# First gate weights of the second token half: raw and combined, into strided free rows of arena H instead of W

## The chip, the cores and the metric

One core of one Trainium2 chip. The metric is the device time of a run in microseconds (us). A time is quoted as the median of several runs, and a profile is one execution out of them.

## The reference, cut to what matters

```
xn = layernorm(A_x)                            # 2048 tokens x 1024
s  = linear_attention(xn, wqkv) @ wo           # 32 heads
g  = silu((silu(xn @ w_gate) * (xn @ w_up)) @ w_down)     # 1024 -> 3584 -> 1024
return A_x + s * g
```

The kernel does all large products with a Strassen-like scheme of seven multiplications, which needs sums and differences of weight blocks. VectorE makes these while TensorE multiplies. The tokens are worked in two halves of 1024.

## The kernel before

Each weight panel is loaded by `wload`: a raw panel of 8 KB per partition, four large sums of it ("combined"), and eight small sums for the inner level of the scheme.

```python
def wload(src, joint, dt=BF16, rd=()):
    s = raw_ring.take()
    dma(list(rd), [s.r], s.ap(dt).rearrange("p (kt n) -> p kt n", n=512), src, dsem("wr%d" % s.k), 1024 * KB)
    v = s.ap(dt).rearrange("p (kt w n) -> p w kt n", w=2, n=256)
    c = cmb_ring.take()
    ...
    sums({...}, [cv[:, q] for q in range(4)], [s.r], cr)        # four large sums
    ...
    for m in joint:                                              # m = 1, 5
        t = in_ring.take()
        ...
        sums(A, [tv[:, q] for q in range(4)], [r], tr)           # four small sums each
```

The buffers lie in arenas: W (52 KB), H (84 KB, the hidden activations), X, P, TM. At the turn from the first token half to the second, the last part of the first half's down projection ("d1") still reads its weights from W, while the first q panel ("q0"), gate panel ("g0") and up panel of the second half must come in:

```python
WD_AT = (((W, 0), (W, 35 * KB), (W, 7 * KB), None), ((W, 14 * KB), (W, 21 * KB), (W, 0), (W, 35 * KB)))
...
raw_ring.__init__([(X, 0), (W, 16 * KB), (W, 0), (X, 0), ...], 8 * KB)        # q0, g0, u0, ...
cmb_ring.__init__([(X, 8 * KB), (W, 28 * KB), (X, 8 * KB)] + ..., 8 * KB)
```

So g0's raw place, W 16 to 24 KB, is taken by d1's weights at 14 and 21 KB until d1's seventh multiplication. The order of instructions on every engine is fixed when the program is built: a planner schedules all operations with modelled durations, and each engine then runs its list in order.

Of the kernel before, what the change touches and what calls it, by code (L numbers as in the profile page):

```python
# [12 lines left out]
BF16 = mybir.dt.bfloat16  # L13
FP16 = mybir.dt.float16
KB = 1024
# [304 lines left out]
def build_kernel(nc, A_x, A_wqkv, A_wo, B_w_gate, B_w_up, B_w_down, out, WINDOW=6, NWARM=15, NPE=2, LEAD=12.0):  # L320
    S, D, FF = 2048, 1024, 3584
    NT, KT, NG, NPAIR = 16, 8, 8, 14
# [5 lines left out]
    wg_v = B_w_gate.rearrange("(kt p) f -> p kt f", p=128)  # L328
    wu_v = B_w_up.rearrange("(kt p) f -> p kt f", p=128)
# [3 lines left out]
    with ExitStack() as es:  # L333
# [20 lines left out]
        def named(*key):  # L354
            return Region([key])

        H = Arena("H", 84 * KB)
        X = Arena("X", 28 * KB)
        P = Arena("P", 16 * KB)
        W = Arena("W", 52 * KB)  # L360
# [50 lines left out]
        def sem(name):  # L411
            return es.enter_context(nc.semaphore(name))
# [4 lines left out]
        def dsem(name):  # L417
            if name not in semn:
                semn[name] = sem("d_" + name)
            return semn[name]  # L420
# [8 lines left out]
        def pe_mm(reads, writes, mms):  # L429
            return PL.op("pe", reads, writes, partial(_mm_group, mms), mm_cost(mms))  # L430
# [21 lines left out]
        def tt(reads, writes, o, a, b, op, fast=False):  # L452
            return dve(reads, writes, lambda h: h.tensor_tensor(o, a, b, op), nel(o), 1.92 if fast else 0.96)  # L453

        def dma(reads, writes, o, i, s, nbytes, cow=None, after=None):
            return PL.op("sp", reads, writes, lambda h: h.dma_start(o, i), 0.47, sem=s,  # L456
                         nbytes=nbytes * (1.45 if nbytes in (128 * KB, 896 * KB) else 1.0), cow=cow,
                         after=after)
# [97 lines left out]
        def combos(v, after=None):  # L556
            for o, a, b in (("T3", "R11", "R01"), ("T1", "R01", "R00"), ("T2", "R11", "T1"), ("T4", "R10", "T2")):
                for h in range(2):
                    w = {}
                    for nm in (o, a, b):  # L560
                        ap, r = v[nm]
                        n = len(r.keys) // 2
                        w[nm] = ap[:, 2 * h:2 * h + 2, :], Region(r.keys[n * h:n * h + n])
                    q = tt([w[a][1], w[b][1]], [w[o][1]], w[o][0], w[a][0], w[b][0], ALU.subtract, True)
                    if after is not None:
                        q.preds.add(after)
                        after.succs.append(q)
# [8 lines left out]
        for n in range(NWARM):  # L576
            b = n % 8
            m = 512 if n > 3 else 128
# [379 lines left out]
        for n, (fn, args) in enumerate(((x_load, (0,)), (x_load, (1,)), (wkv_load, (0, 1, 0)), (wkv_load, (0, 1, 1)),  # L958
# [3 lines left out]
            k = len(PL.ops)  # L962
# [6 lines left out]
        for n in range(6):  # L969
            o = pe_mm(wz_r[:1], [bank_r[kvb[2]]], [(ps[kvb[2]][:, 0:128], wz[:, 0:128], wz[:, 0:128], True, True)])  # L970
# [74 lines left out]
        for q, kb in enumerate(kvb):  # L1045
            n = 3 if q < 2 else 2
            src = ps[kb][:, 0:129 * n].rearrange("p (g n) -> p g n", n=129)[:, :, 128:129]
# [3 lines left out]
        for g in range(NG):  # L1051
            kvp = kv_ap(g)
            dve([bank_r[kvb[g // 3]], zi_r, mask_r], [H.reg(32 * KB + g * 256, 256)],
                lambda h, g=g, kvp=kvp: h.scalar_tensor_tensor(
                    KVZ[:, g, :], kvp[:, 0:128], zinv[:, g:g + 1], maskbd[:, :], ALU.mult, ALU.mult), 128)
# [35 lines left out]
        raw_ring = Places([(W, o * KB) for o in (0, 8, 16)], 8 * KB)  # L1091
        cmb_ring = Places([(W, 24 * KB), (W, 32 * KB)] * 2 + [(W, 24 * KB), (P, 0)] + [(W, 32 * KB), (W, 24 * KB)] * 6, 8 * KB)
        in_ring = Places([(W, 40 * KB), (W, 42 * KB), (W, 44 * KB), (TM, 8 * KB)], 2 * KB)

        def sums(A, o, rd, wr):

            tt(rd, [wr[0]], o[0], A[0, 1], A[1, 1], ALU.add, True)
            tt(rd + [wr[0]], [wr[1]], o[1], o[0], A[0, 0], ALU.subtract, True)
            tt(rd, [wr[2]], o[2], A[0, 0], A[0, 1], ALU.subtract, True)
            tt(rd + [wr[1]], [wr[3]], o[3], A[1, 0], o[1], ALU.subtract, True)  # L1100
# [1 line left out]
        RAW_OF = {1: (0, 0), 2: (1, 0), 4: (1, 1)}  # L1102
        SUM_OF = {5: 0, 6: 1, 7: 2, 3: 3}

        def wload(src, joint, dt=BF16, rd=()):


            s = raw_ring.take()
            dma(list(rd), [s.r], s.ap(dt).rearrange("p (kt n) -> p kt n", n=512), src, dsem("wr%d" % s.k), 1024 * KB)
            v = s.ap(dt).rearrange("p (kt w n) -> p w kt n", w=2, n=256)  # L1110
            c = cmb_ring.take()
            cv = c.ap(FP16).rearrange("p (m w kt n) -> p m w kt n", m=4, w=2, n=128)
            cr = [c.sub(q * 2 * KB, 2 * KB).r for q in range(4)]
            sums({(k, i): v[:, :, 4 * k:4 * k + 4, i * 128:i * 128 + 128] for k in range(2) for i in range(2)},
                 [cv[:, q] for q in range(4)], [s.r], cr)

            def block(m):
                if m in RAW_OF:
                    k, i = RAW_OF[m]
                    return v[:, :, 4 * k:4 * k + 4, i * 128:i * 128 + 128], s.r  # L1120
                return cv[:, SUM_OF[m]], cr[SUM_OF[m]]

            def stat(w, m):
                bl, r = block(m)
                return [bl[:, w, q, :] for q in range(4)], r
            inner = {}
            for m in joint:
                bl, r = block(m)
                t = in_ring.take()
                tv = t.ap(FP16).rearrange("p (m kt n) -> p m kt n", m=4, n=128)  # L1130
                tr = [t.sub(q * KB // 2, KB // 2).r for q in range(4)]
                A = {(k, i): bl[:, i, 2 * k:2 * k + 2, :] for k in range(2) for i in range(2)}
                sums(A, [tv[:, q] for q in range(4)], [r], tr)
                inner[m] = (A, r, tv, tr)

            def jstat(m, k):
                A, r, tv, tr = inner[m]
                if k in RAW_OF:
                    return [A[RAW_OF[k]][:, q, :] for q in range(2)], r
                return [tv[:, SUM_OF[k], q, :] for q in range(2)], tr[SUM_OF[k]]  # L1140
            return stat, jstat
# [116 lines left out]
                tt([sr, zrr], [sr], dst, src, zr, ALU.mult, True)  # L1258


        HB = 6 * KB
        HOF = {"R00": 0, "R10": 1, "R01": 2, "T1": 2, "R11": 3, "T2": 4, "T3": 5}

        def hb(n, nm):
            o = n * HB + HOF[nm] * KB
            return H.at(o, KB, FP16), H.reg(o, KB)

        def hb2(n, nm):

            v = H.at(n * HB, 2 * HB, FP16).rearrange("p (n b t) -> p n b t", n=2, t=512)[:, :, HOF[nm], :]  # L1270
            return v, Region(hb(n, nm)[1].keys + hb(n + 1, nm)[1].keys)

        def gu_load(k, n):
            return wload((wg_v if k == "g" else wu_v)[:, :, n * 512:(n + 1) * 512], (1, 5))

        sgs = {}

# [34 lines left out]
        def h_sums(n):  # L1312
            v = {nm: hb2(n, nm) for nm in HOF}
            tt([v["R11"][1], v["R01"][1]], [v["T3"][1]], v["T3"][0], v["R11"][0], v["R01"][0], ALU.subtract, True)
            tt([v["R01"][1], v["R00"][1]], [v["T1"][1]], v["T1"][0], v["R01"][0], v["R00"][0], ALU.subtract, True)
            tt([v["R11"][1], v["T1"][1]], [v["T2"][1]], v["T2"][0], v["R11"][0], v["T1"][0], ALU.subtract, True)
# [24 lines left out]
        def hq(nm, k, j, u0, u1):  # L1341

            v = H.at(0, NPAIR * HB, FP16).rearrange("p (u k b t) -> p u k b t", k=2, b=6, t=512)
            keys = []
            for u in range(u0, u1):
                keys += H.reg((2 * u + k) * HB + HOF[nm] * KB + j * 512, 512).keys
            return v[:, u0:u1, k, HOF[nm], j * 256:j * 256 + 256], Region(keys)

# [336 lines left out]
        gate = [0]  # L1685
# [16 lines left out]
        def turn_pass():  # L1702

            for q in range(4):
                dma([named("xscr", q)], [P.reg(q * 4 * KB, 4 * KB)], P.at(q * 4 * KB, 4 * KB, FP16), x_scr[q],
                    dsem("xl%d" % q), 512 * KB)
            k = len(PL.ops)
            combos(XV[1])
            x_inner(XV[1])
            for o in PL.ops[k:]:  # L1710
                o.urgent = 6.0
            gate[0] = 1
            raw_ring.__init__([(X, 0), (W, 16 * KB), (W, 0), (X, 0), (W, 8 * KB), (W, 16 * KB)] + [(W, 0), (W, 8 * KB), (W, 16 * KB)] * 5, 8 * KB)
            cmb_ring.__init__([(X, 8 * KB), (W, 28 * KB), (X, 8 * KB)] + [(W, 24 * KB), (W, 32 * KB)] * 8, 8 * KB)
            in_ring.__init__([(W, 14 * KB), (TM, 8 * KB), (W, 24 * KB), (W, 26 * KB), (W, 42 * KB), (W, 44 * KB)]
                             + [(W, 40 * KB), (TM, 8 * KB), (W, 42 * KB), (W, 44 * KB)] * 8, 2 * KB)
            pump(1)
            last_pair[0] = q_pair(1, 0, got["q", 1, 0], {}, False)
            return last_pair[0]
# [104 lines left out]
```

## Time and profile before

| | before |
|---|---|
| median of 3 runs | 712.3 us (711.97 to 712.69) |
| the profiled run | 713.57 us, span 711.8 us |
| TensorE busy | 705.0 us, 99% |
| VectorE busy | 630.9 us, 89% |

In the lines of a profile, PE is TensorE, DVE is VectorE, SPq is the queue that issues transfers, and "ps" is a PSUM buffer, into which TensorE's products go. The chain of that profile, in order of time (start, length, what), has its last two long TensorE pieces here:

```profile
349.45 29.75 PE ps L309 x175
...
416.46 228.48 PE ps L309 x1370
...
644.97 60.97 PE ps L309 x340
```

From the start of the first to the start of the last are 644.97 - 349.45 = 295.52 us. This distance, called "the stretch" below, contains the turn.

### The profile page before, as it was taken

To read this page: it belongs to the slowest core of one execution; us is meant where nothing else is said; L and a number is where in the kernel's file an instruction comes from. 1 tells how busy PE (TensorE), PEld (TensorE's weight loads), DVE (VectorE), ACT (ScalarE), POOL (GpSimd) and SP (SyncE) were. 2 spreads that over 40 slices of the span, in tenths; PEclk is the share of its full clock that TensorE was granted. 3 is DMA by queue.
4 is the path that set the end of the run, shared out by engine and by line. 5 is a ranking of instruction groups with operands and counts; after the bars stand their busy time and mean duration, and the time that the engine had idled before them with its cause. 6 is when DMAs were issued, how large, how long until landed. Compare 5 with 4: busy or idle time off the path is not lost.

```text
span 711.8 us, 11445 instructions
## 1 busy us (share of the span) xinstructions
PE 705.0 (99%) x4181; PEld 387.3 (54%) x4181; DVE 630.9 (89%) x1534; ACT 424.7 (60%) x827; POOL 12.8 (2%) x34
## 2 busy tenths in 40 slices
PE   8999999999999999999999999999999999999997
PEld 4444445555555555556555455555555555565654
DVE  6999858989999999988958989999999999797863
ACT  5788756988679566663212257876886756531212
POOL 2111000000000000000000000000000000000000
PEclk9999999999999999999999999999999999999999
DMA  9654134345664252326499955323715241646763
GB/s 310 133 99 110 30 118 123 116 143 186 187 178 141 95 171 90 119 71 175 120 233 198 215 142 149 107 73 94 207 60 192 76 149 60 184 134 168 136 160 92
DMA packets 140872, 98.66 MB, mean 139 GB/s; under 512 B 34960, under 2 KB 137872, under 8 KB 140816
## 3 DMA queue, kind: packets, MB, share of 16 engines
q1 hardware_dynamic: 139472, 96.69, 49.8%
q10 hardware_dynamic: 1344, 1.25, 0.5%
q8 instruction: 33, 0.54, 0.3%
q14 instruction: 23, 0.19, 0.1%
HBM read 77.59 MB, written 12.71 MB: 127 GB/s over the span
## 4 chain that ended last, share of the span: by engine, by line
PE 93%; DMA 3%; DVE 3%; issue 0%; SPq 0%; ACT 0%; DVEq 0%
PE ps L309 93%; DVE W L453 1%; DMA W<-in_B_w_gate_dram 1%; DMA H<-in_A_wqkv_dram 1%; DMA TM<-TM 1%; DVE TM L453 1%; DVE X L453 0%; DVE ps L453 0%; PE ps L316 0%; DVE P L453 0%; SPq L456 0%; SPq L760 0%; ACT TM L442 0%; SPq L1621 0%; DVEq L301 0%
## 5 line engine op out<-in xcount | busy, mean ns | idle before, releaser
L309 PE MATMUL ps<-X,W 128*128 128x512 f16 (+2 forms) x1372 | 288.8, 350 | 0.0
L442 ACT ACTIVATE TM<-ps 128x512 f16<-128x512 f32 (+3 forms) x386 | 202.8, 554 | 103.9 <-PE ps L309 97.8
L309 PE MATMUL ps<-H,W 128*128 128x512 f16 (+2 forms) x1096 | 218.4, 351 | 0.1
L453 DVE TENSOR_TENSOR W<-W 128x1024 f16<-128x1024 bf16 (+5 forms) x412 | 184.6, 484 | 5.0 <-PE ps L309 2.7
L309 PEld LDWEIGHTS ps<-X,W 128*128 128x128 f16 (+1 forms) x1372 | 132.1, 98 | 103.8 <-ACT H L442 1.0
L309 PEld LDWEIGHTS ps<-H,W 128*128 128x128 f16 (+1 forms) x1096 | 105.8, 98 | 95.3 <-DVE ps L453 1.1
L453 DVE TENSOR_TENSOR ps<-ps,TM 128x256 f32<-128x256 f32 (+1 forms) x250 | 132.5, 531 | 14.4 <-PE ps L309 11.2
L442 ACT ACTIVATE ps<-ps 128x512 f32<-128x512 f32 (+1 forms) x174 | 85.8, 494 | 89.9 <-PE ps L309 89.4
L442 ACT ACTIVATE H<-ps 128x512 f16<-128x512 f32 (+1 forms) x132 | 78.4, 605 | 37.9 <-PE ps L309 37.9
L309 PE MATMUL ps<-P,W 128*128 128x256 f16 (+1 forms) x516 | 99.5, 319 | 0.0
L453 DVE TENSOR_TENSOR H<-H 128x1024 f16<-128x1024 f16 (+5 forms) x126 | 71.9, 585 | 0.6 <-ACT H L442 0.4
L442 ACT ACTIVATE TM<-TM 128x512 f16<-128x512 f32 (+1 forms) x70 | 44.0, 630 | 44.5 <-DVE TM L453 43.4
L309 PEld LDWEIGHTS ps<-P,W 128*128 128x128 f16 (+1 forms) x516 | 50.1, 98 | 29.1 <-ACT TM L442 0.8
L309 PE MATMUL ps<-W 128*128 128x256 f16 (+1 forms) x330 | 62.3, 282 | 0.4 <-DVE ps L453 0.2
L453 DVE TENSOR_TENSOR H<-H,TM 128x512 f16<-128x512 f16 (+1 forms) x120 | 48.4, 420 | 8.5 <-ACT H L442 8.3
L453 DVE TENSOR_TENSOR TM<-ps,TM 128x512 f32<-128x512 f32 (+3 forms) x63 | 41.8, 663 | 12.8 <-PE ps L309 11.9
L309 PEld LDWEIGHTS ps<-W 128*128 128x128 f16 (+1 forms) x330 | 31.3, 98 | 32.6 <-DVE ps L453 1.3
L309 PE MATMUL ps<-H,X 128*128 128x512 bf16 (+1 forms) x150 | 35.2, 379 | 0.5 <-DMA H<-in_A_wqkv_dram 0.5
L453 DVE TENSOR_TENSOR TM<-TM 128x512 bf16<-128x512 f16 (+2 forms) x73 | 29.3, 414 | 7.0 <-ACT TM L442 4.3
L309 PE MATMUL ps<-H,P 128*128 128x512 bf16 (+1 forms) x110 | 26.8, 379 | 0.0
L453 DVE TENSOR_TENSOR H<-ps,TM 128x512 f16<-128x512 f32 (+1 forms) x35 | 24.2, 690 | 2.2 <-PE ps L309 1.3
L453 DVE TENSOR_TENSOR TM<-TM,W 128x512 f16<-128x512 f16 (+1 forms) x39 | 14.2, 369 | 11.4 <-ACT TM L442 11.4
(103 smaller groups left out, 398.7 us busy)
## 6 DMA issues: line engine op xcount, KB each, us to landing
W<-in_B_w_gate_dram SPq DMA_DIRECT2D x14, 1024.0 KB, 5.4
W<-in_B_w_up_dram SPq DMA_DIRECT2D x14, 1024.0 KB, 5.5
W<-in_B_w_down_dram SPq DMA_DIRECT2D x14, 896.0 KB, 6.4
H<-r_scratch SPq DMA_DIRECT2D x32, 128.0 KB, 3.8
W<-m_scratch SPq DMA_DIRECT2D x4, 1024.0 KB, 5.2
s_scratch<-TM SPq DMA_DIRECT2D x32, 128.0 KB, 2.0
TM<-in_A_x_dram SPq DMA_DIRECT2D x16, 256.0 KB, 3.5
W<-in_A_x_dram SPq DMA_DIRECT2D x15, 256.0 KB, 3.4
```

The costliest lines, as they stand in the source:

```text
L309: last = h.matmul(o, l, r, start=st, stop=sp, skip_group_check=True)
L442: q = PL.op("act", reads, writes, lambda h: h.activation(o, i, func, **kw), nel(o) / (1000.0 if "bias" in kw or not isinstance(kw.get("sca ...
L453: return dve(reads, writes, lambda h: h.tensor_tensor(o, a, b, op), nel(o), 1.92 if fast else 0.96)
```

## The change: its intent, and the diff

The rows of H that hold hidden blocks R00 and T1 are dead once d1's two inner products are done, long before the end of d1. The change loads g0's raw weights into R00 of eight blocks, 6 KB apart, and puts its four large sums into T1. So the load can go out earlier.

```diff
+        def strips(nm, dt):
+            return (H.at(0, NPAIR * HB, dt).rearrange("p (n b t) -> p n b t", b=6, t=512)[:, 0:8, HOF[nm], :],
+                    [hb(n, nm)[1].keys for n in range(8)])
+
+        def wload(src, joint, dt=BF16, rd=(), inh=(0, 0)):
+            if inh[0]:
+                sv, keys = strips("R00", dt)
+                sr = Region(sum(keys, ()))
+                sem = dsem("wrh")
...
+            if inh[0]:
+                ld.urgent = 6.0
...
+            if inh[1]:
+                cs, keys = strips("T1", FP16)
...
-            return wload(..., (1, 5))
+            return wload(..., (1, 5), inh=(1, 1) if gate[0] and (k, n) == ("g", 0) else (0, 0))
...
-            raw_ring.__init__([(X, 0), (W, 16 * KB), (W, 0), (X, 0), ...
-            cmb_ring.__init__([(X, 8 * KB), (W, 28 * KB), (X, 8 * KB)] + ...
+            raw_ring.__init__([(X, 0), (W, 0 * KB), (X, 0), ...
+            cmb_ring.__init__([(X, 8 * KB), (X, 8 * KB)] + ...
```

More of the change, by code (lines that the diff above doesn't have):

```diff
@@ L1093, in build_kernel, with hb @@
         in_ring = Places([(W, 40 * KB), (W, 42 * KB), (W, 44 * KB), (TM, 8 * KB)], 2 * KB)
+        HB = 6 * KB
+        HOF = {"R00": 0, "R10": 1, "R01": 2, "T1": 2, "R11": 3, "T2": 4, "T3": 5}
+        def hb(n, nm):
+            o = n * HB + HOF[nm] * KB
+            return H.at(o, KB, FP16), H.reg(o, KB)
         def sums(A, o, rd, wr):
@@ L1103, in build_kernel @@
         SUM_OF = {5: 0, 6: 1, 7: 2, 3: 3}
-        def wload(src, joint, dt=BF16, rd=()):
-            s = raw_ring.take()
-            dma(list(rd), [s.r], s.ap(dt).rearrange("p (kt n) -> p kt n", n=512), src, dsem("wr%d" % s.k), 1024 * KB)
-            v = s.ap(dt).rearrange("p (kt w n) -> p w kt n", w=2, n=256)
-            c = cmb_ring.take()
-            cv = c.ap(FP16).rearrange("p (m w kt n) -> p m w kt n", m=4, w=2, n=128)
-            cr = [c.sub(q * 2 * KB, 2 * KB).r for q in range(4)]
+        def strips(nm, dt):
[6 more added lines that the diff above has]
+                sem = dsem("wrh")
+            else:
+                s = raw_ring.take()
+                sv, sr, sem = s.ap(dt).rearrange("p (kt n) -> p kt n", n=512), s.r, dsem("wr%d" % s.k)
+            ld = dma(list(rd), [sr], sv, src, sem, 1024 * KB)
+            if inh[0]:
+                ld.urgent = 6.0
+            v = sv.rearrange("p kt (w n) -> p w kt n", n=256)
+            if inh[1]:
+                cs, keys = strips("T1", FP16)
+                cv = cs.rearrange("p (m w) (kt n) -> p m w kt n", w=2, n=128)
+                cr = [Region(keys[2 * q] + keys[2 * q + 1]) for q in range(4)]
+            else:
+                c = cmb_ring.take()
+                cv = c.ap(FP16).rearrange("p (m w kt n) -> p m w kt n", m=4, w=2, n=128)
+                cr = [c.sub(q * 2 * KB, 2 * KB).r for q in range(4)]
             sums({(k, i): v[:, :, 4 * k:4 * k + 4, i * 128:i * 128 + 128] for k in range(2) for i in range(2)},
-                 [cv[:, q] for q in range(4)], [s.r], cr)
+                 [cv[:, q] for q in range(4)], [sr], cr)
             def block(m):
@@ L1119, in block @@
                     k, i = RAW_OF[m]
-                    return v[:, :, 4 * k:4 * k + 4, i * 128:i * 128 + 128], s.r
+                    return v[:, :, 4 * k:4 * k + 4, i * 128:i * 128 + 128], sr
                 return cv[:, SUM_OF[m]], cr[SUM_OF[m]]
@@ L1258, in normalise_part @@
                 tt([sr, zrr], [sr], dst, src, zr, ALU.mult, True)
-        HB = 6 * KB
-        HOF = {"R00": 0, "R10": 1, "R01": 2, "T1": 2, "R11": 3, "T2": 4, "T3": 5}
-        def hb(n, nm):
-            o = n * HB + HOF[nm] * KB
-            return H.at(o, KB, FP16), H.reg(o, KB)
         def hb2(n, nm):
@@ L1273, in gu_load @@
         def gu_load(k, n):
-            return wload((wg_v if k == "g" else wu_v)[:, :, n * 512:(n + 1) * 512], (1, 5))
+            return wload((wg_v if k == "g" else wu_v)[:, :, n * 512:(n + 1) * 512], (1, 5), inh=(1, 1) if gate[0] and (k, n) == ("g", 0) else (0, 0))
         sgs = {}
@@ L1712, in turn_pass @@
             gate[0] = 1
-            raw_ring.__init__([(X, 0), (W, 16 * KB), (W, 0), (X, 0), (W, 8 * KB), (W, 16 * KB)] + [(W, 0), (W, 8 * KB), (W, 16 * KB)] * 5, 8 * KB)
-            cmb_ring.__init__([(X, 8 * KB), (W, 28 * KB), (X, 8 * KB)] + [(W, 24 * KB), (W, 32 * KB)] * 8, 8 * KB)
+            raw_ring.__init__([(X, 0), (W, 0 * KB), (X, 0), (W, 8 * KB), (W, 16 * KB)] + [(W, 0), (W, 8 * KB), (W, 16 * KB)] * 5, 8 * KB)
+            cmb_ring.__init__([(X, 8 * KB), (X, 8 * KB)] + [(W, 24 * KB), (W, 32 * KB)] * 8, 8 * KB)
             in_ring.__init__([(W, 14 * KB), (TM, 8 * KB), (W, 24 * KB), (W, 26 * KB), (W, 42 * KB), (W, 44 * KB)]
```

## The prediction

> **What bounds the kernel now.** I began with the page: is any engine the bound over the whole span?
>
> ```profile
> span 711.8 us, 11445 instructions
> PE 705.0 (99%) x4181; PEld 387.3 (54%) x4181; DVE 630.9 (89%) x1534; ACT 424.7 (60%) x827; POOL 12.8 (2%) x34
> PEclk9999999999999999999999999999999999999999
> PE 93%; DMA 3%; DVE 3%; issue 0%; SPq 0%; ACT 0%; DVEq 0%
> ```
>
> TensorE is busy 99% of the span at full clock, and 93% of the chain that ended last is matmuls. The change neither adds nor removes a matmul, so all it can win or lose is time in which TensorE waits. The list of who waited for whom, TensorE's rows only, says how much is recorded:
>
> ```profile
> PE ps L309 <- DVE TM L574: 1.0, 1, 1.0
> PE ps L309 <- DVE ps L453: 0.9, 2, 0.6
> PE ps L316 <- DVE TM L453: 0.6, 1, 0.6
> PE ps L309 <- DMA H<-in_A_wqkv_dram: 0.5, 1, 0.5
> PE ps L309 <- DVE W L453: 0.2, 1, 0.2
> ```
>
> Columns: total wait, times, longest. The first, third and fourth rows are the start and the last microseconds, which the diff doesn't touch. The two that remain, 0.9 + 0.2 us, all fall between 400 and 420 us, the turn from the first token half's down projection (its second column half, "d1") to the second half's first q pair ("q0") and first gate pair ("g0"). That is the place of the change. The chain in order of time shows that this is also the one long stretch in which the chain leaves TensorE (379 to 416 us). Its end:
>
> ```profile
> 402.40 0.62 DVE X L453
> 403.01 0.19 SPq L1621
> 403.20 0.04 issue
> 403.25 8.07 DMA W<-in_B_w_gate_dram
> 411.32 0.02 issue
> 411.34 3.70 DVE W L453 x12
> ```
>
> After them come one more W sum (0.69 us at 415.37), a PSUM add (0.35 us at 416.06), and TensorE again at 416.46. So the gate load of g0 lands at 411.32, VectorE then does g0's sums, and q0's PSUM add stands behind them. TensorE's timeline over that stretch (start, length, last in brackets the wait):
>
> ```profile
> 406.35 1.03 PE L309 MATMUL ps<-W 128*128 128x512 f16 x4
> 407.62 0.39 PE L309 MATMUL ps<-W 128*128 128x256 f16 x2 [0.24 <-DVE ps L453]
> ...
> 411.31 2.02 PE L309 MATMUL ps<-W 128*128 128x512 f16 x8
> 413.50 1.04 PE L309 MATMUL ps<-W 128*128 128x512 f16 x4 [0.17 <-DVE W L453]
> ...
> 414.59 1.25 PE L309 MATMUL ps<-P,X 128*128 128x256 f16 x6
> 416.46 0.39 PE L309 MATMUL ps<-W,TM 128*128 128x256 f16 x2 [0.62 <-DVE ps L453]
> ```
>
> The bracketed waits understate the loss, since matmuls overlap. In the unbroken run 408.06 to 410.65 us twelve 512-column matmuls take 2.59 us, 0.216 each; a pair of 256-column ones takes 0.22 (402.46 to 402.68). With this spacing the three stalls are:
> - 407.62 - (406.35 + 4 x 0.216) = 0.41 us
> - 413.50 - (411.31 + 8 x 0.216) = 0.46 us
> - 416.46 - (414.59 + 6 x 0.11) = 1.21 us
>
> Together 2.1 us: 0.3% of 712.3 us is the ceiling for the change at this place. VectorE's timeline tells what stood before the second and third stall:
>
> ```profile
> 411.34 0.29 DVE L453 TENSOR_TENSOR W<-W 128x256 f16<-128x256 bf16 x1 [1.52 <-DMA W<-in_B_w_gate_dram]
> 411.55 0.69 DVE L453 TENSOR_TENSOR W<-H 128x1024 f16<-128x1024 f16 x1
> 412.15 0.69 DVE L453 TENSOR_TENSOR W<-W 128x1024 f16<-128x1024 bf16 x1
> 412.75 0.68 DVE L453 TENSOR_TENSOR W<-H 128x1024 f16<-128x1024 f16 x1
> 413.36 2.70 DVE L453 TENSOR_TENSOR W<-W 128x256 f16<-128x256 f16 x9
> 415.97 0.43 DVE L453 TENSOR_TENSOR ps<-ps,TM 128x256 f32<-128x256 f32 x1
> ```
>
> VectorE runs in program order. It idled 1.52 us for the gate load with the W<-H subtractions standing behind it. These make d1's last moving operand, for which TensorE waits at 413.50. Then g0's sums hold back q0's PSUM add at 415.97, for which it waits at 416.46. The order is fixed when the program is built, by a planner with its own durations; it evidently expected the load earlier than it came.
>
> **What the Trainium skill says.** "Perfetto Trace Analysis", section "Tensor Engine Instruction (MATMUL, LD_WEIGHTS)", says that the profiled end of a matmul is estimated from its size. The trace agrees: 512-column matmuls are recorded at 379 ns and start 216 ns apart; hence my use of start times. "VectorE: DVE Perf Modes", section "Mode 2×_1P", asks for 16-bit data in unit steps, 4-byte aligned. The strided rows keep 128 or more adjacent elements, so the mode should hold. The trace agrees for a like case: W<-H subtractions, whose two rows in H lie 6 KB apart, take a median 687 ns, against 695 ns for X<-X of the same size inside contiguous blocks. "DMA: Bandwidth & Descriptors", section "Issuing engines are not separate DMA queues", says that all transfers interleave on the same 16 engines. The gate load of g0 took 8.1 us to land and another one, issued at 433.9 us, 5.5 us, which fits competition at the turn.
>
> **The change part by part.**
> 1. *Destination of g0's load*: from W at 16 to 24 KB to rows R00 of the first eight hidden blocks in H. In W, that place holds d1's down weights until its last step 7, which TensorE leaves about 402.5 us. R00 is last read by d1's first inner product (the last of its steps reads P and W at 374.1 us). So the buffer is free from about 375 us instead of 402.5. I expect the issue later than that, because the planner ties a load to a matmul 12 us before its deadline. Deadline: g0's first matmul is near 420.6 us by my reading; less some 2 us for sums, less 9.2 us that the planner allows for 1 MB, less the new urgency of 6, less 12: about 391. Issue at 388 to 395 us, landing with 6 to 8 us at 395 to 402. No bytes change, and each contiguous run stays 1 KB.
> 2. *Destination of g0's four large sums*: from W at 28 to 36 KB to rows T1, free after d1's second inner product (last matmul of it about 387.3 us). In W, the last kilobyte of that block overlaps d1's last down weights, in use until about 414.4 us, so the fourth sum had to come late; that goes too. Durations stay.
> 3. *g0's eight small sums*, also with unchanged places (W 24 and 26 KB), still wait for step 7 of d1, 402.5 us. They can run soon after.
> 4. *Rings*: the later loads get the places they had; only g0's two entries are gone.
>
> VectorE's work for g0 is 4 x 0.60 + 8 x 0.20 = 4.0 us (spacings of such sums at 398.15 to 399.35 us). It is moved, not saved. In 411.0 to 416.5 VectorE was busy 5.16 of 5.50 us; 4.0 less leaves about 1.2. In 403 to 411 it was busy 5.80 of 8.00, so 2.2 us are free there for the displaced sums, and the rest fit between 411 and 416.5. Stalls two and three, 0.46 + 1.21 = 1.67 us, should go. Stall one comes from q0's PSUM add at 407.13, behind a wait of 0.72 us for a transpose and an X sum; neither is part of the change, so I count none of its 0.41.
>
> Gain 1.67 us; I take off about 0.4 for stalls that the new order makes elsewhere. 712.3 - 1.3 = 711.0 us.
>
> **Rivals.**
> - *Another wait takes its place.* From 395 to 403 VectorE was busy 8.00 of 8.00 us with sums that q0 needs. A megabyte loading near 391 joins the transposes and x loads on queues with a share of about 1.1 there; a late transpose holds VectorE (it already did for 0.75 us at 392.8), and q0 starts later. For it: that full stretch, and the 7 us a transpose takes. Against: the chain has slack until the end of the down projection's matmuls, and g0's sums have late deadlines, so they should not go first. It would give back 1 to 2 us: 711.7 to 713.
> - *All three stalls go*, because with the load out of 403 to 411 the transposes land sooner. Then 710.2.
> - *The plan reshuffles elsewhere.* Everything after the turn is planned anew; small hidden waits may come or go. Weight loads wait 1.6 us on PSUM adds between 416 and 700 us, 1.1 of it at the turn itself, so there is little to win later; some tenths to lose.
> - *Strided rows slow the weight loads or sums.* Nothing in the trace speaks for it; doubling the four sums would cost 2.4 us of VectorE, half hidden: about 712.
>
> **Range and chances.** Centre 711.0. The ceiling bounds the low side: 712.3 - 2.1 = 710.2, less 0.2 for the spread of the runs (711.97 to 712.69), so 710.0. The high side is rival one at half strength: 712.5. A 2% move would be 14 us, against 2.1 us to be had and no mechanism for a loss so large unless the new plan is badly off.
>
> **What would show it.** Right: gate load issued before 396 us and no VectorE wait on it; no TensorE waits at 413 and 416; g0's large sums inside H before 411; VectorE's busy time the same within 2 us. Wrong: load still issued after 400; a TensorE wait on q0's first weights near 402; a longer transpose wait on VectorE between 390 and 405; new TensorE waits after 420; sums into H longer than 0.7 us.

## The result, and the profile after

| | before | after |
|---|---|---|
| median of 6 runs | 712.31 us (711.47 to 712.72) | 712.2 us (711.41 to 714.5) |
| the profiled run | 713.57 us | 711.96 us |
| span of the profile | 711.8 us | 710.2 us |
| the stretch | 295.52 us | 293.85 us |

The ratio is 1.0003, with a 95% interval from 0.9988 to 1.0018. (A ratio is the mean time of one kernel's fast runs over that of the other's of the same rounds, so it isn't quite the ratio of the medians quoted.) The time didn't change, though the two profiles differ by 1.6 us in span and by 1.67 us in the stretch.

In the changed kernel the chain stays on TensorE through the turn. From its page and its chain in order of time:

```profile
span 710.2 us, 11444 instructions
PE 98%; DMA 1%; SPq 0%; issue 0%; DVE 0%; ACT 0%
```

```profile
349.88 293.82 PE ps L309 x1732
643.70 0.03 issue
643.73 60.97 PE ps L309 x340
```

The queue that issues transfers sends g0's load at 391.00 us (it was 403.25), and it lands 5.6 us later, at 396.6. VectorE's timeline shows the first g0 sum at 404.46 without a wait, and the four large sums (H<-H) at 406.35 and from 412.10:

```profile
391.00 0.40 SPq L456 DMA_DIRECT2D H<-in_B_w_gate_dram  x1
```

```profile
404.46 0.28 DVE L453 TENSOR_TENSOR W<-H 128x256 f16<-128x256 bf16 x1
406.35 0.68 DVE L453 TENSOR_TENSOR H<-H 128x1024 f16<-128x1024 bf16 x1
412.10 1.89 DVE L453 TENSOR_TENSOR H<-H 128x1024 f16<-128x1024 f16 x3
```

TensorE's timeline has no bracketed wait left at the turn:

```profile
411.33 2.75 PE L309 MATMUL ps<-W 128*128 128x512 f16 x12
413.93 0.38 PE L309 MATMUL ps<-W,TM 128*128 128x256 f16 x2
414.14 1.25 PE L309 MATMUL ps<-P,X 128*128 128x256 f16 x6
415.23 0.38 PE L309 MATMUL ps<-W,TM 128*128 128x256 f16 x2
```

The twelve matmuls from 411.33 run through where the old profile broke at 413.50. Nothing is left of the old third stall either. A row of the timeline joins matmuls of different shape, and shows the shape of the first; asked by shape, the row of six at 414.14 is

```profile
L309 PE MATMUL ps<-P,X 128*128 128x512 f16 x4 | 1.0, 379 | 0.0
L309 PE MATMUL ps<-P,X 128*128 128x256 f16 x2 | 0.4, 272 | 0.0
```

So it takes 2 x 0.11 + 4 x 0.216 = 1.08 us, and 414.14 + 1.08 = 415.22 is where the next row starts. The row of six at 414.59 in the old profile is made up in the same way; the prediction counted it as six of the small shape.

So the profile did what was foretold and the time did not follow. Three theories:
- **A**: the first profile of before caught an unlucky run, in which the gate load landed late; in most runs of before there is no stall to remove.
- **B**: before loses 1.7 us in every run, and the changed kernel gives its gain back somewhere.
- **C**: the gain is there in the mean, under the noise of the timing.

### The profile page after: what moved, and what is told of

It is laid out like the page before. It is cut to its first block, busy times and chain, and to the rows that moved or that the text cites. A ratio compares the mean times of both kernels' runs of the same rounds, so it can differ in the third digit from the quotient of the medians.

```text
span 710.2 us, 11444 instructions
## 1 busy us (share of the span) xinstructions
PE 704.5 (99%) x4181; PEld 388.1 (55%) x4181; DVE 631.2 (89%) x1534; ACT 424.9 (60%) x827; POOL 13.0 (2%) x34
## 4 chain that ended last, share of the span: by engine, by line
PE 98%; DMA 1%; SPq 0%; issue 0%; DVE 0%; ACT 0%
PE ps L309 98%; DMA H<-in_A_wqkv_dram 1%; PE ps L316 0%; DVE TM L453 0%; SPq L456 0%; SPq L760 0%; ACT TM L442 0%
## 5 line engine op out<-in xcount | busy, mean ns | idle before, releaser
L309 PE MATMUL ps<-X,W 128*128 128x512 f16 (+2 forms) x1348 | 282.6, 349 | 0.0
L309 PEld LDWEIGHTS ps<-X,W 128*128 128x128 f16 (+1 forms) x1348 | 130.0, 98 | 101.6 <-ACT H L442 1.0
L453 DVE TENSOR_TENSOR W<-W 128x256 f16<-128x256 f16 (+5 forms) x400 | 178.8, 479 | 2.7 <-PE ps L309 1.9
L309 PE MATMUL ps<-P,W 128*128 128x256 f16 (+1 forms) x492 | 94.5, 318 | 0.0
L453 DVE TENSOR_TENSOR H<-H 128x1024 f16<-128x1024 f16 (+5 forms) x130 | 73.7, 581 | 0.7 <-ACT H L442 0.5
L309 PEld LDWEIGHTS ps<-P,W 128*128 128x128 f16 (+1 forms) x492 | 47.9, 98 | 27.0 <-ACT TM L442 0.8
```

The lines of the kernel that those rows point to most:

```text
L309: last = h.matmul(o, l, r, start=st, stop=sp, skip_group_check=True)
L453: return dve(reads, writes, lambda h: h.tensor_tensor(o, a, b, op), nel(o), 1.92 if fast else 0.96)
```

## The experiments

**More profiles of the kernel before, and the changed kernel again.** No edit.

> The kernel before, unchanged, run against itself: it gives the noise of the comparison and a second profile of the turn. In the first profile TensorE lost 2.1 us in three stalls between 402 and 417 us, and that profiled run took 713.57 us, 1.3 us over the median of the other runs. Theory A (that profile was an unlucky sample: the gate load landed late in it, 8.1 us): the stalls of this profile sum to 1.2 us or less, with the gate load landing within 7 us, and the ratio is 1.000 within 0.001. Theory B (the 2.1 us are lost in every run, and the changed kernel gives its gain back somewhere): the stalls are 1.8 to 2.3 us again. Theory C (the gain is there and lies under the noise of the timing): stalls as in B, and the ratio of these two equal kernels differs from 1 by 0.001 or more.

> The changed kernel again, in more rounds. A: no stall between 402 and 417 us in its profile, ratio 0.9985 to 1.0. B: ratio 1.000 within 0.0005 although the stalls are gone. C: ratio 0.997 to 0.9985, the gain of 1.2 to 2.1 us that the two profiles showed.

Measured: before against itself 0.9998 (0.9985 to 1.0010); the changed kernel 0.9999 (0.9986 to 1.0011), median 711.86 us against 711.96. The second profile of before, its chain in order of time:

```profile
349.89 293.81 PE ps L309 x1732
643.71 0.03 issue
643.74 60.97 PE ps L309 x340
```

The stretch is 293.85 us, as in the changed kernel to the hundredth. And on its VectorE the first g0 sum, which waited 1.52 us in the first profile, has no wait in brackets:

```profile
409.17 0.69 DVE L453 TENSOR_TENSOR W<-H 128x1024 f16<-128x1024 f16 x1 [0.27 <-PE ps L309]
409.77 0.29 DVE L453 TENSOR_TENSOR W<-W 128x256 f16<-128x256 bf16 x1
```

The load was issued at 403.1 us, as in the first profile, but landed after 6.2 us instead of 8.1. Issue and landing in the second profile:

```profile
403.10 0.39 SPq L456 DMA_DIRECT2D W<-in_B_w_gate_dram  x1
DMA to landing us min/median/max: 6.2/6.2/6.2
```

Theory A holds here, and B falls: there was nothing to give back.

> The kernel before, a third profile. Theory A: no stall at the turn, with the gate load landing in 6 to 6.5 us; if it lands in 7 us or more there is a stall of about the lateness over 409.8 us.

> The kernel before, a fourth profile: the same as the third. If two of the four profiles had stalls of 1 us or more, the stall is common, and the change should gain several tenths of a microsecond on average; if only the first has, it is rare.

> The kernel before, a fifth profile. Theory A: the stretch is 293.82 us within 0.03 and the load lands within 6.6 us of its issue; if it lands later, the stretch is longer.

> The kernel before, a sixth profile. From the profiles so far: TensorE's stretch between its two fixed points (the starts of its last two long pieces in the chain) is 293.85 us when the gate load lands up to 60.2 us after the first of them, and longer by exactly the excess otherwise. Theory A: 293.85, landing at 59.0 to 59.8; or, if it is the rare case, a longer stretch that obeys this line within 0.1 us. Theory B (stall in most runs): longer than 294.5.

> The same, a seventh profile: how often the load is late is all that is asked. One in five so far.

> The same, an eighth profile. If none of the three has a stall, the rate is one in eight, and the mean gain to expect of the change is 1.67 us times an eighth, 0.2 us, which no comparison made here can resolve.

Measured: stretches of 293.85, 293.84, 293.84, 293.84, 293.84 and 293.84 us; the load landed 5.5 to 6.6 us after its issue. So one profile of eight of the kernel before has the stall. The runs themselves took 711.86 to 713.33 us, so what varies in them lies elsewhere: in the sixth profile the stretch began at 351.24 us (349.13 to 349.89 in the others of these six), and in the third the part after the stretch took 68.3 us (711.3 - 642.98) against 66.5 in the seventh. The sixth also has a TensorE wait of 0.5 us in the first token half, which the change doesn't touch: an up panel took 10.1 us to land near 190 us. (So had the profile with combined sums alone, below: 10.4 us and a wait of 0.8.)

```profile
180.05 10.08 DMA W<-in_B_w_up_dram
```

This load is late more often than g0's. In five of the eighteen profiles of this case, of both kernels, it landed 9.4 to 10.4 us after its issue and the chain runs through it; in the other thirteen it took 8.2 to 9.2 us and the chain stays on TensorE there. From the start of the chain's long TensorE piece near 125 us to the start of the stretch, those five took 224.46 to 225.42 us, against 224.16 in the second profile. No run here moves this load.

**The two halves of the change alone.** Raw weights only in H, and combined weights only in H (each with the old ring for the other half):

```diff
-            ... inh=(1, 1) if gate[0] and (k, n) == ("g", 0) else (0, 0))
+            ... inh=(1, 0) if gate[0] and (k, n) == ("g", 0) else (0, 0))      # e3; (0, 1) in e4
```

> Only the raw gate weights go to H (with the earlier load); the combined ones stay in W at 28 to 36 KB. If the early load is what removed the stalls, the profile shows no stall or at most 0.4 us at the turn, as the changed kernel. If the combined sums in W held the fourth sum back behind the end of the down projection, a stall of 0.5 us or more near 415 us remains. Time within 0.1% of the changed kernel either way.

> Only the combined weights go to H; the raw load still goes to W at 16 to 24 KB, near 403 us. If the load is the cause, VectorE still waits for it near 410 us and TensorE has stalls at the turn as before (A: 0.4 to 2.1 us, changing from run to run with the landing of the load). If the place of the sums was the cause, the stalls are gone. Time within 0.1% of the kernel before.

Measured: 1.0002 (0.9989 to 1.0015) and 0.9999 (0.9986 to 1.0013). Both profiles have a stretch of 293.85 us. With the combined sums alone the load lands 6.1 us after its issue and nothing waits for it. As the kernel before has no stall in most runs either, these two can't tell which half would remove it; that they can't is itself what theory A says. The place of the combined sums in W costs nothing visible: the stall of 0.5 us that the second explanation in the expectation asked for is not there.

**A late load on purpose.** An extra memory-to-memory transfer goes into the queue just ahead of g0's load, after planning, so that the order on the compute engines stays the same:

```diff
         PL.schedule()
+        o = Op()                       # sem of its own, waits for d1's last seventh multiplication
+        o.fn = lambda h: h.dma_start(junk[0][:, :], B_w_gate[0:1024, 0:512])      # 1 MB; 256 or 512 rows in e9, e10
+        PL.order.insert(where, o)      # before: ahead of g0's load; changed kernel: the same place of the queue
```

> The kernel before with one extra transfer of 1 MB, memory to memory, in the queue just ahead of g0's gate load; the order of all instructions on the compute engines is the same. In the second profile of before, the load landed at 409.3 us and VectorE reached it at 409.8 without waiting, so the slack was about 0.5 us; 1 MB at the 330 to 380 GB/s seen in the busiest slices is about 3 us. Theory A (a stall at the turn comes when, and only when, the load lands later than about 409.8): the load lands near 412.3, VectorE waits 2 to 3 us, TensorE loses 2 to 3.5 us at the turn, ratio 1.003 to 1.005. Rival (the slack of the turn is larger, the stalls of the first profile came from something else, such as the late transposes): ratio within 0.001 of 1.

> The changed kernel with the same extra 1 MB at the same place of the queue. Theory A: g0's load landed near 397 us, so nothing waits for the extra transfer but transposes; stalls at the turn 0 to 0.5 us, ratio to before 0.999 to 1.001, and so 0.2 to 0.4% faster than the kernel before with the extra transfer. Rival (late transposes made the stalls): as slow as the other.

> The kernel before with an extra 256 KB (instead of 1 MB) ahead of g0's gate load. With 1 MB the load landed 9.4 us after its issue, 3.2 us later than without. A quarter should add about 0.8 us, landing near 7.0 us after issue, which is 0.3 to 0.5 us beyond the slack. Theory A: TensorE's stretch from 349 to 643 us, 293.82 us in all profiles without a stall, grows by 0.2 to 0.8 us. Rival (slack much larger than 0.5 us): 293.8 again. The time moves by less than the noise of 0.15%.

> The same with 512 KB: landing near 7.8 us after issue, like the 8.1 us of the first profile of before. Theory A: the stretch grows by 1.0 to 1.7 us (it was 295.52, 1.70 more, in the first profile), no drop of the clock[...]. If the late transposes of the first profile, not the gate load, made its stalls, the stretch grows by less than 0.7.

With 1 MB, before took a median of 714.09 us, ratio 1.0020 (1.0000 to 1.0040), and the changed kernel with the same transfer 712.14 us, ratio 0.9992 (0.9974 to 1.0009); the median of the plain kernel in these rounds was 712.85. The loss was smaller than expected (a ratio of 1.003 to 1.005), and the two intervals overlap; but all six runs of the one took 713.37 us or more, and five of six of the other 712.86 or less. The changed kernel has no wait for it and a stretch of 293.86 us. In the kernel before, VectorE waits and then TensorE. The profiled run took 717.22 us and was the slowest of its six, so what it lost is more than the usual loss. VectorE's and TensorE's timelines of that run:

```profile
412.87 0.29 DVE L453 TENSOR_TENSOR W<-W 128x256 f16<-128x256 bf16 x1 [3.35 <-DMA W<-in_B_w_gate_dram]
```

```profile
411.01 1.03 PE L309 MATMUL ps<-W 128*128 128x512 f16 x4
413.82 1.04 PE L309 MATMUL ps<-W 128*128 128x512 f16 x4 [1.79 <-DVE W L453]
415.03 1.79 PE L309 MATMUL ps<-W 128*128 128x512 f16 x4 [0.17 <-DVE W L453]
416.61 0.64 PE L309 MATMUL ps<-W,TM 128*128 128x256 f16 x2
417.04 2.01 PE L309 MATMUL ps<-P,X 128*128 128x256 f16 x6
418.88 0.38 PE L309 MATMUL ps<-W,TM 128*128 128x256 f16 x2
```

It is the picture of the first profile, larger. The smaller transfers were a miss as a dose: with 256 KB the load took 8.4 us (7.0 expected), with 512 KB 6.7 (7.8 expected). Their medians were 713.72 us, ratio 1.0015 (0.9997 to 1.0032), and 713.79 us, ratio 1.0018 (1.0001 to 1.0035). The stretch with 512 KB grew by only 0.41 us, and under 0.7 was to speak for the late transposes; but the load hadn't come as late as that test assumed, so the test doesn't decide. The landing varies by more than these sizes add in a single profile. But each profile is a measured landing with a measured stretch, and so better than the dose. Their chains hold the landing, here with 512 KB and with 256 KB:

```profile
403.54 6.74 DMA W<-in_B_w_gate_dram
...
415.42 228.48 PE ps L309 x1370
643.89 0.03 issue
643.92 60.97 PE ps L309 x340
```

```profile
403.01 8.43 DMA W<-in_B_w_gate_dram
...
416.58 228.48 PE ps L309 x1370
645.06 0.03 issue
645.09 60.97 PE ps L309 x340
```

The stretches began at 349.66 and 349.13. All in one table, landing counted from the start of the stretch:

| profile of the kernel before | landing | stretch over 293.85 | landing less excess |
|---|---|---|---|
| second | 59.4 us | 0.00 us | |
| seventh | 59.8 us | 0.00 us | |
| with 512 KB ahead | 60.62 us | 0.41 us | 60.21 |
| first | 61.87 us | 1.67 us | 60.20 |
| with 256 KB ahead | 62.31 us | 2.11 us | 60.20 |
| with 1 MB ahead | 63.29 us | 3.98 us | 59.31 |

Up to about 60.2 us a landing costs nothing; past it every microsecond of lateness is a microsecond of time. (Three profiles lie on this line to 0.01 us; none has a landing between 59.8 and 60.6.) The last row loses some 0.9 us more, and the windows of that run, with the granted clock (the column PEclk), show why:

```profile
413.80:416.00 2.20, 2.01 (x7) 0.72 (x8) 2.20 (x8) 0.00 (x0) 0.00 (x0) 0.81 0.74 204
416.00:418.00 2.00, 2.00 (x8) 1.01 (x7) 1.88 (x5) 1.72 (x3) 0.00 (x0) 0.50 0.19 53
418.00:420.00 2.00, 2.00 (x12) 1.01 (x11) 1.50 (x5) 1.67 (x3) 0.00 (x0) 0.86 0.86 253
```

After the gaps TensorE ran at half clock. If the clock is either full or half, the three means give 0.84, 2.00 and 0.56 us at half: 3.4 us together. That leaves 1.7 us of work undone. The third stall, 0.79 us in the first profile, is swallowed by it (the row of six at 417.04 takes longer, and the next at 418.88 has no wait), and 0.9 us is left over.

**A late load in the changed kernel.** The extra 1 MB directly ahead of g0's load near 391 us (same edit, another place):

> The changed kernel with the extra 1 MB directly ahead of its own gate load, near 391 us. Theory A: the load lands near 400 us instead of 396.6, its first use on VectorE is near 404.5, so nothing waits for it, and the ratio to before is 0.999 to 1.001. Rival one of the prediction (the load's neighbourhood in the queue is crowded: the transposes behind it come late and hold VectorE): a VectorE wait for a transpose of 0.5 us or more between 393 and 406 us; if that reaches TensorE, the stretch is longer than 293.9.

> The changed kernel with the extra 1 MB ahead of its gate load, a second profile: its first took 713.81 us where its other five runs took 715.2 to 718.9. If the drop of the clock after a gap of 2 us or more makes the difference, this profile shows either a granted clock of 0.8 or less for some 2 us after the gap with a time over 715, or no drop with a time near 713.8.

Measured: 1.0052 (1.0031 to 1.0073), median 715.62 us. Theory A as I had extended it to this case failed. The gate load did land in time: at 399.6 us, with its first sum at 406.25. But the transposes of d1's outputs, which stand behind it in the queue, came late, and they hold VectorE ahead of q0's sums. First profile, VectorE and TensorE:

```profile
401.83 0.43 DVE L453 TENSOR_TENSOR TM<-TM 128x512 bf16<-128x512 f16 x1 [2.18 <-DMA TM<-TM]
```

```profile
409.49 0.39 PE L309 MATMUL ps<-W 128*128 128x256 f16 x2 [2.00 <-DVE ps L453]
```

The second profile took 720.37 us, with two VectorE waits for transposes of 6.0 us in sum, TensorE waits of 3.71 and 2.75 us, and the half clock after the first of them:

```profile
410.40 0.61 PE L309 MATMUL ps<-W 128*128 128x512 f16 x2 [3.71 <-DVE TM L453]
413.76 0.61 PE L309 MATMUL ps<-W 128*128 128x256 f16 x2 [2.75 <-DVE ps L453]
```

```profile
410.00:412.00 2.00, 0.61 (x2) 0.11 (x2) 2.00 (x6) 1.12 (x2) 0.00 (x0) 0.79 0.07 11
412.00:414.00 2.00, 0.24 (x2) 0.19 (x3) 2.00 (x6) 0.00 (x0) 0.00 (x0) 0.50 0.32 66
414.00:416.00 2.00, 2.00 (x8) 0.99 (x7) 1.36 (x5) 0.58 (x1) 0.00 (x0) 0.50 0.76 197
416.00:418.00 2.00, 2.00 (x7) 0.62 (x6) 0.89 (x2) 0.00 (x0) 0.00 (x0) 0.50 0.23 66
```

This is the prediction's first rival. It isn't active in the changed kernel (no VectorE wait for a transpose between 385 and 418 us in its profile), but 1 MB more in that place wakes it. In the first of the two profiles the clock stayed full after a gap of 2.0 us and the run took 713.81 us. Of the 6.6 us between the two, longer waits are the larger part: 3.71 + 2.75 - 2.00 = 4.5 us. The half clock lasted 6.8 us by the same working, but TensorE worked in only 4.2 us of it (from 413.76 to about 418.0), so some 2.1 us are its share, an estimate.

## Why the prediction was wrong

**The bound and its place**: right. TensorE's waits are all there is to win, and the turn is where the change acts; the 1.67 us between the two first profiles lie in the stretch.

**The baseline**: this step failed. The prediction wrote "712.3 - 1.3 = 711.0 us". It took stalls measured in one run, the profiled one, from the median of other runs. The profiled run had taken 713.57 us. Like with like gives 713.57 - 1.67 = 711.90 us, and the profiled run of the changed kernel took 711.96. A run 1.3 us slower than the median, whose profile shows 1.7 us of stalls caused by a transfer that took 8.1 us where a later one took 5.5, is a hint that the stalls are what made it slow. I cited the 8.1 us and read it as the rule of that place. Seven more profiles show 5.5 to 6.6 us there and no stall.

**The size of the gain in that run**: 1.67 us foretold, 1.67 us found (295.52 - 293.85), but by two errors that cancel, so by luck. Stall one (0.41 us), of which I counted nothing, vanished as well. Stall three was mis-sized: its row of six holds two matmuls of 256 columns and four of 512, so it was 416.46 - (414.59 + 2 x 0.11 + 4 x 0.216) = 0.79 us, not 1.21. The three stalls were 0.41 + 0.46 + 0.79 = 1.66 us, not 2.1, and all three are gone, as the prediction's second rival had it. But they are gone from the second profile of the kernel before as well, so their going isn't shown to be the work of the change.

**Part 1, the load**: right. Issue foretold at about 391, found at 391.00; landing foretold at 395 to 402, found at 396.6. **Parts 2 and 3, the sums**: durations right (0.68 us in the strided rows of H, VectorE busy 631.2 us against 630.9), time wrong: three of the four large sums run after 412 us, not before 411, and do no harm there. **Part 4**: right.

**The deduction of 0.4 us for new stalls elsewhere**: not needed; the stretch of the changed kernel equals that of an undisturbed run of before to 0.01 us.

**What the change really does**: it moves slack. In seven of eight profiles of before, the load lands 0.4 to 1.0 us ahead of the point where lateness begins to cost (59.2 to 59.8 against 60.2). In the changed kernel it lands 7.9 us ahead of its first use (396.6 to 404.46). With 1 MB of extra traffic late at the turn the changed kernel stays at 712.14 us and the other goes to 714.09. A mean gain of 1.67/8 = 0.2 us, if one run in eight is late, is an estimate from these profiles; theory C at that size can't be excluded, and none of the comparisons, with intervals of 0.12 to 0.2% (0.9 to 1.4 us) to either side, could see it.

**What stays open**: why the transfers were slow in the first profile. It wasn't the gate load alone: the seven transposes between 383 and 412 us took a median of 5.0 us to land, against 3.2 in the second profile, and the transfer engines were busier (a share of 1.26 against 0.95 between 383 and 390 us) for as many GB/s (261 against 270). Nothing in the kernel differs between the two.

## What to carry to other kernels

Before a stall in a profile is counted as a gain, compare the time of the profiled run with the median of the unprofiled ones; if it is slower by about the stall, take a second profile first. Measure the distance between two fixed points on the bound engine, not the span: here it repeats to 0.01 us where whole runs scatter by 1 us and more. And for a transfer near its deadline, ask for its slack: moving it earlier buys nothing while it is in time, and may spend the slack of others that stand behind it in the queue.

## What the Trainium skill lacked or had wrong

- "TensorE: Matmul & The Clock Gate", section "What's actually happening", has in its table the half clock after at least one idle window of about 3.4 us. In the kernel before with 1 MB ahead, it came after a gap of 1.95 us (413.82 less 411.01 + 4 x 0.216), followed by a second of 0.35 us; in the first profile of the changed kernel with 1 MB ahead of its load, one gap of 2.2 us (2.00 us as recorded) left the clock full. So gaps shorter than the window were enough in one profile, and one wasn't in another. The length of the half-clock phase, 3.4 us as worked out above, agrees with the page's window; in the second profile of the changed kernel with that transfer it was 6.8 us, twice the window.
- No page read for this says how much the landing of one and the same transfer varies from run to run: 1 MB with a median of 5.4 us over the kernel took 5.5 to 8.1 us at this one place in eight profiles.
